# Column-normalised attention with a soft mixture of experts on one core: two PSUM sums of squares, seven more split tiles, another written order

## The chip, the cores and the metric

One Trainium2 chip, one core of it. The metric is device time in microseconds (us) of one launch. Five engines work beside each other and are named as in the profile: PE (TensorE, matmuls; PEld is its weight load), DVE (VectorE), ACT (ScalarE), POOL (GpSimd) and SP (SyncE, which here issues every DMA).

## The reference

Four batches of 5056 tokens with 256 channels, all fp32. Attention is over the channels: the columns of q and k are normalised over the tokens, and their product is a 256 x 256 matrix per batch. The result of all batches goes through a soft mixture of 8 experts with 4 slots each.

```python
qn = q / (np.linalg.norm(q, axis=1, keepdims=True) + 1e-06)
kn = k / (np.linalg.norm(k, axis=1, keepdims=True) + 1e-06)
s = kn.transpose(0, 2, 1) @ qn / tau
a = softmax(s, axis=-1)
x = (v @ a).reshape(20224, 256)
logits = x @ phi                      # 32 slots
d = softmax(logits, axis=0)           # over all tokens
slot_input = d.T @ x                  # 32 x 256
h = np.maximum(slot_input[e] @ w1[e], 0.0);  slot_out[e] = h @ w2[e]
c = softmax(logits, axis=1)
out = c @ slot_out
```

x is never formed: per batch, M = a @ phi gives the logits as v @ M, and the slots are gathered as (d.T @ v) @ a.

## The kernel before

**Tiling.** q and k of a batch come in 10 units (u = 0 to 39 over the four batches) of up to four tiles of 128 tokens; a unit is one 1 MB load, `raw`. A tile j of a unit goes one of two ways. As it is, it costs PE one fp32 product per half of the columns (L316, `S<-raw`). Split (j below `NS[u]`), ACT casts it to fp32r (L271, `hl<-raw`), POOL subtracts the cast from the original for the rest (L275), and PE makes three fp32r products per half (L322, `S<-hl`). Before, NS splits 108 tiles: none of unit 0, two in units 1 to 9, three in all later ones. ACT also squares the whole unit (L279, `sq<-raw`), and DVE adds the squares of all tiles of a batch in one PSUM bank, `A` (L286 for the first add of two tiles, then L298), the last add going to SBUF as `nsum` (L296). PE sums `nsum` over the partitions (L335, `nn`), and the norms, the scaled scores, their exponentials `a` and M follow on DVE, POOL, ACT and PE.

v comes in 20 pairs p (five a batch, one 1 MB load each). The logits need v transposed, `x`: for the pairs in `LT` it is loaded a second time in turned form (1 MB, L454), for the other seven PE turns v in 16 transposes (L459, `T`) and ACT copies the four banks to `x` (L464). PE makes the logits (L479, `L`), running maxima go over DVE and PE, and PE gathers v with the weights into the slots (L593, `G`). After the last batch come the experts (L742 `H`, L760, L775 `O`) and then the output: PE (L813), copies by ACT and DVE (L830) into 21 MB of stores by SP (L834 to L839).

**What sets the order.** Every step is a Python function put into the list `plan`; `ORDER` is a permutation of that list, written out by hand, and `run(plan)` calls the steps in that order. Each engine executes its instructions in just this order; semaphores make one wait for another. `SLOTS` gives every large tile one of 22 SBUF buffers of 1 MB, `BANKS` every PSUM tile one of 8 banks. A load or a step that takes a buffer waits until the tile that had it before has been read for the last time, and everything behind it on its engine waits with it. SP issues the loads in one queue, so a load that waits holds up the ones behind it.

`constants` makes the identity on POOL, a few constants and the sums `fold`, `fold4` from the identity on DVE (L231, L233), and a first Exp on ACT (`warm`). It stands 18th in the order before: POOL makes the identity after its first two subtractions.

Of the kernel before, what the change touches and what calls it, by code (L numbers as in the profile page):

```python
# [24 lines left out]
NT = [3 if u % (2 * UB) == 2 * UB - 1 else 4 for u in range(NU)]  # L25

NS = [0, 2, 2, 2, 2, 2, 2, 2, 2, 2, 3, 3, 3, 3, 3, 3, 3, 3, 3, 3, 3, 3, 3, 3, 3, 3, 3, 3, 3, 3, 3, 3, 3, 3, 3, 3, 3, 3, 3, 3]

LT = {0, 1, 2, 3, 4, 5, 6, 7, 8, 9, 10, 11, 12}
# [6 lines left out]

ORDER = [
# [130 lines left out]
def colnorm_attention_soft_moe(  # L168
# [112 lines left out]
    def add(u, j):  # L281
        b, i = divmod(u, UB)
        s = sqs[u].rearrange("p j x c -> p j (x c)")
        if i == 0 and j == 1:
            st[b]["acc"] = bank(f"A{b}")
            dve.tensor_tensor(st[b]["acc"], s[:, 0], s[:, 1], op=ALU.add)  # L286
            return
        r = slice(0, P)
        if j == 3 and i == UB - 1:
            r = slice(0, HD)  # L290
        elif j < 0:
# [767 lines left out]
```

## Time and profile before

| what | us |
|---|---|
| runs of the kernel | 302.66, 303.75, 623.18 (median 303.75) |
| the profiled execution, its own time | 302.02 |
| its span, first to last instruction | 300.1 |
| PE / DVE / ACT / POOL busy in the span | 256.4 / 222.1 / 201.7 / 143.5 |
| data moved | 113.96 MB, 92.57 MB of it read |

The span falls in three parts: the inputs with all of the attention up to some 227 us, the experts to some 245, and the output to the end. A row of the profile names line, engine, operation, the tile written and those read; "waits" are idle stretches of an engine, put down to what ended them. A line number is that of the kernel printed above.

### The profile page before, as it was taken

The page shows a single profiled execution, that of the slowest core. Times are in us where ns is not written, and L with a number is a line of the kernel's source. Part 1 is how long each engine was busy: PE and PEld are TensorE (multiplying, and loading weights), DVE is VectorE, ACT ScalarE, POOL GpSimd, SP SyncE. Part 2 cuts the span into 40 slices and gives each one's busy share as a digit, 9 for nine tenths or more (in the row PEclk, how much of TensorE's full clock was granted, in tenths as well). Part 3 has the DMA queues.
Part 4 walks back from the last instruction along what each step waited for, and adds up shares of the span by engine and source line. Part 5 has one row for each costly group of instructions (what it writes and reads, how often), then busy time and mean ns, then how long its engine had stood idle before and what let it go on. Part 6 is the DMA issues. An engine that isn't in the chain of part 4 may idle for free.

```text
span 300.1 us, 6394 instructions
## 1 busy us (share of the span) xinstructions
PE 256.4 (85%) x2526; PEld 202.9 (68%) x2526; DVE 222.1 (74%) x432; ACT 201.7 (67%) x302; POOL 143.5 (48%) x118
## 2 busy tenths in 40 slices
PE   5699799998999996999799988999989999997000
PEld 3498699997777885986667776877753777764000
DVE  0299489899948799999999999938889447884200
ACT  2995998959888995966878761859733327675000
POOL 0678699995797998777947963000000000000000
PEclk9999899999999999999999999999997999999555
DMA  7999999999999999999999999999993019999996
GB/s 286 425 425 421 420 419 330 340 405 371 428 421 420 416 425 424 420 412 418 418 421 423 419 420 419 419 421 420 420 420 128 2 72 382 415 416 417 419 423 264
DMA packets 16446, 113.96 MB, mean 380 GB/s; under 512 B 1952, under 2 KB 1952, under 8 KB 3488
## 3 DMA queue, kind: packets, MB, share of 16 engines
q1 hardware_dynamic: 16416, 113.55, 92.2%
q8 instruction: 20, 0.33, 0.4%
q14 instruction: 10, 0.08, 0.1%
HBM read 92.57 MB, written 20.97 MB: 378 GB/s over the span
## 4 chain that ended last, share of the span: by engine, by line
PE 39%; DVE 18%; POOL 16%; issue 9%; ACT 8%; DMA 2%; SPq 0%; DVEq 0%; POOLq 0%; ACTq 0%
POOL hl L275 15%; DVE A L298 9%; PE op_None L813 6%; PE S L322 5%; ACT sq L279 5%; PE G L593 4%; PE T L459 4%; PE L L479 4%; PE H L742 3%; PE S L316 3%; PE O L775 3%; PE op L813 2%; DMA raw<-in_qk_dram 2%; ACT hl L271 2%; ACT o L830 1%
## 5 line engine op out<-in xcount | busy, mean ns | idle before, releaser
L275 POOL TENSOR_TENSOR hl<-raw,hl 128x512 fp32r<-128x512 f32 x108 | 139.0, 1323 | 36.0 <-ACT hl L271 36.0
L298 DVE TENSOR_TENSOR A<-sq,A 128x512 f32<-128x512 f32 (+1 forms) x148 | 101.6, 691 | 10.1 <-ACT sq L279 5.6
L322 PE MATMUL S<-hl 128*128 128x256 f32 x648 | 93.5, 295 | 2.0 <-POOL hl L275 1.3
L322 PEld LDWEIGHTS S<-hl 128*128 128x128 f32 x648 | 83.0, 192 | 9.2 <-issue 4.9
L279 ACT ACTIVATE sq<-raw 128x2048 f32<-128x2048 f32 (+1 forms) x40 | 75.2, 1888 | 7.9 <-DVE A L298 5.3
L316 PE MATMUL S<-raw 128*128 128x256 f32 (+1 forms) x208 | 55.7, 403 | 6.5 <-DMA raw<-in_qk_dram 6.5
L271 ACT CAST hl<-raw 128x1024 fp32r<-128x1024 f32 (+1 forms) x69 | 56.4, 855 | 3.4 <-PE S L316 1.2
L316 PEld LDWEIGHTS S<-raw 128*128 128x128 f32 (+1 forms) x208 | 38.2, 198 | 15.6 <-DMA raw<-in_qk_dram 8.7
L830 DVE COPY o<-op_None 128x512 f32<-128x512 f32 x30 | 19.1, 685 | 6.9 <-PE op_None L813 5.9
L813 PE MATMUL op_None<-so,cT 32*128 32x256 f32 x240 | 23.0, 411 | 1.0 <-ACT o L830 0.6
L593 PE MATMUL G<-v,dn 128*32 128x256 f32 x312 | 19.5, 382 | 3.5 <-DVE dn L573 3.1
L830 ACT COPY o<-op_None 128x512 f32<-128x512 f32 x30 | 16.0, 593 | 7.4 <-PE op_None L813 7.0
L813 PEld LDWEIGHTS op_None<-so,cT 32*128 32x128 f32 x240 | 16.1, 183 | 7.1 <-ACT o L830 4.0
L479 PE MATMUL L<-x,M 128*32 128x256 f32 (+1 forms) x320 | 20.3, 380 | 0.4 <-ACT M L424 0.4
L593 PEld LDWEIGHTS G<-v,dn 128*32 128x32 f32 x312 | 10.4, 109 | 9.6 <-issue 3.6
L464 ACT COPY x<-T 128x512 f32<-128x512 f32 x28 | 14.9, 604 | 2.3 <-PE T L459 2.3
L502 ACT COPY lt<-L 128x256 f32<-128x256 f32 x20 | 7.1, 380 | 12.1 <-PE L L479 10.2
L459 PE MATMUL T<-ident,v 128*128 128x128 f32 x108 | 14.0, 276 | 0.0
L459 PEld LDWEIGHTS T<-ident,v 128*128 128x128 f32 x108 | 11.9, 141 | 2.0 <-issue 1.5
L479 PEld LDWEIGHTS L<-x,M 128*32 128x32 f32 x320 | 9.2, 109 | 6.0 <-ACT M L424 0.9
L830 DVE COPY oh<-op 128x256 f32<-128x256 f32 x20 | 7.3, 416 | 4.7 <-PE op L813 4.6
L563 ACT ACTIVATE lt<-lt,negm 128x256 f32<-128x256 f32 (+2 forms) x11 | 7.5, 682 | 4.8 <-DVE negm L547 4.7
(113 smaller groups left out, 249.2 us busy)
## 6 DMA issues: line engine op xcount, KB each, us to landing
raw<-in_qk_dram SPq DMA_DIRECT2D x37, 1024.0 KB, 12.9
v<-in_v_dram SPq DMA_DIRECT2D x16, 1024.0 KB, 10.7
w<-in_moe_w_dram SPq DMA_DIRECT2D x16, 1024.0 KB, 12.6
out_dram<-o SPq DMA_DIRECT2D x15, 1024.0 KB, 12.7
x<-in_vt_dram SPq DMA_DIRECT2D x13, 1024.0 KB, 11.8
out_dram<-oh SPq DMA_DIRECT2D x4, 1024.0 KB, 5.8
v<-in_v_dram SPq DMA_DIRECT2D x4, 896.0 KB, 12.9
raw<-in_qk_dram SPq DMA_DIRECT2D x2, 768.0 KB, 9.3
```

The source lines that it names most:

```text
L271: act.copy(parts(u, lo, hi)[:, :, 0::2, :], raws[u][:, lo:hi])
L275: pool.tensor_tensor(hl[:, :, 1::2, :], raws[u][:, lo:hi], hl[:, :, 0::2, :].bitcast(F32), op=ALU.subtract)
L279: act.activation(sqs[u][:, : NT[u]], raws[u][:, : NT[u]], AF.Square)
L298: dve.tensor_tensor(a[r], s[r, j], a[r], op=ALU.add)
L316: pe.matmul(sm, raw[r, j, 1, cols], raw[r, j, 0, :], start=first, stop=False, skip_group_check=True)
L322: pe.matmul(sm, hl[:, w, cols], hl[:, y, :], start=first, stop=False, skip_group_check=True)
L459: pe.transpose(tp[:, P * jj : P * jj + P], vtile(p, 4 * h + jj)[:, P * m : P * m + P], ident)
L464: to(xt(p)[:, m, h * UT : h * UT + UT], tps[p, h, m])
L479: pe.matmul(L[S * g : S * g + S, :n, :], M[:, m, :], x[:, :n, S * g : S * g + S], start=m == 0 and g not in void, stop=m == 1, skip_group_ ...
L593: pe.matmul(gp[S * g : S * g + S, :C], dn[:, x, j, :], vtile(p, j), start=x == 0 and j < G, stop=x == n - 1 and j >= G,)
L813: pe.matmul(ops[b, p, hf, g][:, h, :], cT[b][r, 4 * i : 4 * i + 4, :].rearrange("s j t -> s (j t)"), rhs[r], start=True, stop=True,)
L830: (dve.tensor_copy if g % 2 else act.copy)(dst, ops[b, p, hf, g])
```

## The change

- **Two sums.** The squares of the even and odd tiles of a batch are added in two PSUM banks, `A<b>_0` and `A<b>_1`. In the batch's ninth unit the odd sum goes to SBUF (`nsum<b>_odd`, in the same buffer as `nsum` and `aT`), and a new step `join` adds it to the even one. The last unit's tiles all go to the even bank. There are 156 such additions on DVE before and after.
- **Constants first.** `constants` stands second in the order, behind one load.
- **Split tiles.** NS is 0, 2, 2 and then 3 throughout: 115 tiles split instead of 108. The seven are in units 3 to 9.
- **Pairs.** LT holds the pairs 2 to 14 instead of 0 to 12: 13 turned loads as before, but PE turns the pairs 0 and 1 (and 15 to 19) instead of 13 and 14 (and 15 to 19).
- **Order.** ORDER, SLOTS and BANKS are other tables throughout; the gathers keep their bank under a key of batch and group.

```diff
-NS = [0, 2, 2, 2, 2, 2, 2, 2, 2, 2, 3, 3, 3, 3, 3, 3, 3, 3, 3, 3, 3, 3, 3, 3, 3, 3, 3, 3, 3, 3, 3, 3, 3, 3, 3, 3, 3, 3, 3, 3]
+NS = [0, 2, 2, 3, 3, 3, 3, 3, 3, 3, 3, 3, 3, 3, 3, 3, 3, 3, 3, 3, 3, 3, 3, 3, 3, 3, 3, 3, 3, 3, 3, 3, 3, 3, 3, 3, 3, 3, 3, 3]
-LT = {0, 1, 2, 3, 4, 5, 6, 7, 8, 9, 10, 11, 12}
+LT = {2, 3, 4, 5, 6, 7, 8, 9, 10, 11, 12, 13, 14}
 ORDER = [
-    1, 8, 3, 2, 9, 4, 25, 12, 35, 26, 29, 34, 28, 22, 51, 64, 38, 0, 5, 116, 27, 90, 77, 60, 103, 13, 15, 23,
+    37, 0, 1, 3, 7, 2, 38, 42, 39, 48, 41, 40, 10, 4, 5, 52, 54, 53, 6, 63, 44, 57, 9, 56, 24, 11, 82, 67,
...
     def add(u, j):
...
-        if i == 0 and j == 1:
-            st[b]["acc"] = bank(f"A{b}")
-            dve.tensor_tensor(st[b]["acc"], s[:, 0], s[:, 1], op=ALU.add)
+        if i == 0 and j in (1, 3):
+            st[b]["acc", j // 2] = bank(f"A{b}_{j // 2}")
+            dve.tensor_tensor(st[b]["acc", j // 2], s[:, j - 1], s[:, j], op=ALU.add)
             return
-        r = slice(0, P)
+        r, x = slice(0, P), j % 2 if i < UB - 1 else 0
...
-        a = st[b]["acc"]
-        if i == UB - 1 and j == 2:
+        a = st[b]["acc", x]
+        if i == UB - 2 and j == 3:
+            st[b]["odd"] = bpool.tile([P, 2 * C], F32, tag="nsum", name=f"nsum{b}_odd")
+            dve.tensor_tensor(st[b]["odd"], s[:, j], a, op=ALU.add)
+        elif i == UB - 1 and j == 2:
...
+    def join(b):
+        a = st[b]["acc", 0]
+        dve.tensor_tensor(a, st[b]["odd"], a, op=ALU.add)
...
-    at(-2, constants)
+    at(-9, constants)
...
+        if i == UB - 1:
+            at(u + 0.39, join, b)
```

In the rows of the order below, a name's last number only tells tiles of one program apart; `raw3_93` is the load of unit 3, `sq3` its squares, `A0_0` the even sum of batch 0.

**The start of DVE.** The first instructions behind the memsets, before:

```order
L231 TENSOR_REDUCE fold_81<-ident_72 128x32
L233 COPY fold4_82<-fold_81 128x32 x4
L286 TENSOR_TENSOR A0_139<-sq0_102 128x512
L298 TENSOR_TENSOR A0_139<-sq2_143,A0_139 128x512
L298 TENSOR_TENSOR A0_139<-sq0_102,A0_139 128x512
L298 TENSOR_TENSOR A0_139<-sq1_162,A0_139 128x512
L298 TENSOR_TENSOR A0_139<-sq4_167,A0_139 128x512 x3
L298 TENSOR_TENSOR A0_139<-sq1_162,A0_139 128x512
```

and now:

```order
L230 TENSOR_REDUCE fold_81<-ident_72 128x32
L232 COPY fold4_82<-fold_81 128x32 x4
L285 TENSOR_TENSOR A0_0_131<-sq0_129 128x512
L285 TENSOR_TENSOR A0_1_138<-sq0_129 128x512
L300 TENSOR_TENSOR A0_0_131<-sq3_125,A0_0_131 128x512
L300 TENSOR_TENSOR A0_0_131<-sq2_170,A0_0_131 128x512
L300 TENSOR_TENSOR A0_0_131<-sq4_155,A0_0_131 128x512
L300 TENSOR_TENSOR A0_0_131<-sq3_125,A0_0_131 128x512
L300 TENSOR_TENSOR A0_1_138<-sq4_155,A0_1_138 128x512
L300 TENSOR_TENSOR A0_0_131<-sq4_155,A0_0_131 128x512
L300 TENSOR_TENSOR A0_1_138<-sq4_155,A0_1_138 128x512
L300 TENSOR_TENSOR A0_1_138<-sq6_210,A0_1_138 128x512
```

The sums from the identity stay in front of the first add on DVE; what moved is the identity itself, which POOL now makes before all subtractions. Of the first ten additions before, all but the first read the sum that the one in front of them wrote; now the chain is broken where `A0_1` stands between two of `A0_0`. Over the whole program an addition stands directly behind one whose result it reads 103 times before and 54 times now.

**The start of ACT.** The first instructions before:

```order
L279 ACT_TABLE_LOAD
L279 ACTIVATE sq0_102<-raw0_93 128x2048
L271 CAST hl1_110<-raw2_104 128x4x256
L230 ACTIVATE warm_77<-ones_73 128x1
L279 ACTIVATE sq2_143<-raw2_104 128x2048
L271 CAST hl0_153<-raw1_106 128x4x256
L279 ACTIVATE sq1_162<-raw1_106 128x2048
```

and now:

```order
L229 ACT_TABLE_LOAD
L229 ACTIVATE warm_77<-ones_73 128x1
L270 CAST hl2_117<-raw3_93 128x4x256
L270 CAST hl3_120<-raw3_93 128x2x256
L278 ACTIVATE sq3_125<-raw3_93 128x2048
L278 ACTIVATE sq0_129<-raw0_110 128x2048
L270 CAST hl4_135<-raw4_133 128x4x256
```

The table load and `warm` stand in front of everything that needs data, and the first work is the cast of unit 3, not the square of unit 0. Up to the copy of batch 0's score matrix S0 out of PSUM (`ssb`, L330), ACT has 16 squares, 16 casts of two tiles and 8 of one before; now 15 squares, 15 casts of two tiles, 12 of one and 3 copies of turned v. Behind that copy PE has 77 split tiles, 23 whole ones and 28 banks of transposes before; now 83, 21 and 22.

**PE in front of unit 27.** `raw27` takes a buffer over. Before, it is the buffer of `hl23`, whose last reader is `S1<-hl23` 36 rows ahead of `S2<-raw27` in PE's order; the rows that lie last ahead of `raw27` are:

```order
L593 MATMUL G0_0_957<-v2_654,dn0_0_923 32x256 x8
L322 MATMUL S2_870<-hl28_988 128x256 x6
L322 MATMUL S2_870<-hl29_906 128x256 x6
L316 MATMUL S2_870<-raw26_816 128x256 x2
L322 MATMUL S2_870<-hl27_1029 128x256 x6
L316 MATMUL S2_870<-raw25_784 128x256 x2
L322 MATMUL S2_870<-hl31_996 128x256 x6
L322 MATMUL S2_870<-hl30_994 128x256 x6
L316 MATMUL S2_870<-raw27_821 128x256 x2
```

Now the buffer is that of `v1`, whose last reader is the gather in the first of these rows:

```order
L599 MATMUL G0_0_1027<-v1_309,dn0_0_1025 32x256 x8
L599 MATMUL G0_0_1027<-v2_720,dn0_0_1025 32x256 x8
L328 MATMUL S2_845<-hl28_939 128x256 x6
L328 MATMUL S1_373<-hl27_821 128x256 x6
L328 MATMUL S2_845<-hl33_1059 128x256 x6
L328 MATMUL S2_845<-hl31_1091 128x256 x6
L328 MATMUL S2_845<-hl27_821 128x256 x6
L328 MATMUL S2_845<-hl28_939 128x256 x6
L531 MATMUL rp0_1_1155<-ident_72,mx0_1_1151 1x128
L328 MATMUL S1_373<-hl26_827 128x256 x6
L322 MATMUL S2_845<-raw27_1110 128x256 x2
```

The same holds in kind for the loads of units 20 to 28: between the step that frees the buffer and the first step that needs the new load there is less work on PE than before. (For unit 27 it is now the gather of v2's pair, seven split tiles and one small matmul.)

## Rows read from the trace of the kernel before

**Rows 1.** The page's busy time, share of the span and instructions of each engine, and of its 40 slices (7.5 us each) the busy tenths of the DMA engines and their GB/s.

```profile
PE 256.4 (85%) x2526; PEld 202.9 (68%) x2526; DVE 222.1 (74%) x432; ACT 201.7 (67%) x302; POOL 143.5 (48%) x118
...
DMA  7999999999999999999999999999993019999996
GB/s 286 425 425 421 420 419 330 340 405 371 428 421 420 416 425 424 420 412 418 418 421 423 419 420 419 419 421 420 420 420 128 2 72 382 415 416 417 419 423 264
```

**Rows 2.** Busy time of each engine in four stretches of the span (us from its start; in brackets the number of instructions), granted clock, DMA share, GB/s.

```profile
10.00:62.00 52.00, 48.20 (x293) 42.92 (x291) 40.82 (x61) 45.85 (x38) 45.48 (x38) 0.97 0.99 396
...
190.00:227.00 37.00, 35.79 (x438) 25.78 (x440) 28.75 (x85) 24.64 (x66) 0.00 (x0) 0.99 1.01 417
227.00:245.00 18.00, 18.00 (x326) 10.68 (x322) 9.29 (x18) 6.37 (x12) 0.00 (x0) 0.93 0.04 16
245.00:300.00 55.00, 29.69 (x426) 22.14 (x414) 26.34 (x52) 21.46 (x49) 0.00 (x0) 0.79 0.93 383
```

**Rows 3.** The page's chain that ended last: shares of the span by engine and by line.

```profile
PE 39%; DVE 18%; POOL 16%; issue 9%; ACT 8%; DMA 2%; SPq 0%; DVEq 0%; POOLq 0%; ACTq 0%
POOL hl L275 15%; DVE A L298 9%; PE op_None L813 6%; PE S L322 5%; ACT sq L279 5%; PE G L593 4%; PE T L459 4%; PE L L479 4%; PE H L742 3%; PE S L316 3%; PE O L775 3%; PE op L813 2%; DMA raw<-in_qk_dram 2%; ACT hl L271 2%; ACT o L830 1%
```

**Rows 4.** The same chain in order of time: start in us, us, what.

```profile
28.78 4.16 issue
...
225.24 1.39 DVE cm L687
226.79 8.39 PE H L742 x64
```

**Rows 5.** ScalarE in order of time: start, us, line, operation, out<-in, count, and in brackets the idle time before it and what ended it.

```profile
5.71 1.28 ACT L279 ACT_TABLE_LOAD   x1 [5.71 <-DMA raw<-in_qk_dram]
7.01 1.91 ACT L279 ACTIVATE sq<-raw 128x2048 f32<-128x2048 f32 x1
...
28.25 3.71 ACT L279 ACTIVATE sq<-raw 128x2048 f32<-128x2048 f32 x2 [3.44 <-DVE A L298]
...
62.33 0.65 ACT L330 COPY ssb<-S 128x256 f32<-128x256 f32 x2 [1.53 <-PE S L316]
```

**Rows 6.** VectorE in order of time, columns as in the group before.

```profile
12.98 0.38 DVE L231 TENSOR_REDUCE fold<-ident 128x32 f32<-128x128 f32 x1 [11.75 <-POOL ident masks.py:199]
13.40 2.18 DVE L233 COPY fold<-fold 128x32 f32<-128x32 f32 x4
15.49 0.69 DVE L286 TENSOR_TENSOR A<-sq 128x512 f32<-128x512 f32 x1
16.29 15.56 DVE L298 TENSOR_TENSOR A<-sq,A 128x512 f32<-128x512 f32 x21
...
137.66 0.68 DVE L296 TENSOR_TENSOR nsum<-sq,A 128x512 f32<-128x512 f32 x1
138.25 0.69 DVE L298 TENSOR_TENSOR A<-sq,A 128x512 f32<-128x512 f32 x1
...
178.16 5.13 DVE L298 TENSOR_TENSOR A<-sq,A 128x512 f32<-128x512 f32 x7
```

**Rows 7.** Groups of instructions by line, engine, operation and shape: count, busy us, mean ns of one, idle us of the engine before them and what ended it.

```profile
L275 POOL TENSOR_TENSOR hl<-raw,hl 128x512 fp32r<-128x512 f32 x108 | 139.0, 1323 | 36.0 <-ACT hl L271 36.0
L298 DVE TENSOR_TENSOR A<-sq,A 128x512 f32<-128x512 f32 x144 | 98.9, 691 | 10.0 <-ACT sq L279 5.6
L322 PE MATMUL S<-hl 128*128 128x256 f32 x648 | 93.5, 295 | 2.0 <-POOL hl L275 1.3 <-ACT hl L271 0.6
...
L279 ACT ACTIVATE sq<-raw 128x2048 f32<-128x2048 f32 x38 | 72.2, 1910 | 7.9 <-DVE A L298 5.3 <-POOL hl L275 1.2 <-PE S L322 0.9
L316 PE MATMUL S<-raw 128*128 128x256 f32 x192 | 51.3, 403 | 6.5 <-DMA raw<-in_qk_dram 6.5
L271 ACT CAST hl<-raw 128x1024 fp32r<-128x1024 f32 x39 | 40.2, 1041 | 3.4 <-PE S L316 1.2 <-DVE A L298 1.1 <-issue 0.5
...
L593 PE MATMUL G<-v,dn 128*32 128x256 f32 x312 | 19.5, 382 | 3.5 <-DVE dn L573 3.1 <-issue 0.4
...
L271 ACT CAST hl<-raw 128x512 fp32r<-128x512 f32 x30 | 17.7, 614 | 0.0
...
L464 ACT COPY x<-T 128x512 f32<-128x512 f32 x28 | 14.9, 604 | 2.3 <-PE T L459 2.3
L459 PE MATMUL T<-ident,v 128*128 128x128 f32 x108 | 14.0, 276 | 0.0
```

**Rows 8.** Who waited for whom: us in total, times, longest.

```profile
PE G L593 <- DVE dn L573: 3.1, 2, 2.5
...
PE rp L525 <- DVE mx L520: 1.9, 1, 1.9
...
PE nn L335 <- DVE nsum L296: 1.3, 2, 0.8
```

**Rows 9.** The page's DMA issues (KB each, median us from issue to landing), and the first store in SP's own order of time.

```profile
raw<-in_qk_dram SPq DMA_DIRECT2D x37, 1024.0 KB, 12.9
...
out_dram<-oh SPq DMA_DIRECT2D x4, 1024.0 KB, 5.8
...
245.52 0.35 SPq L839 DMA_DIRECT2D out_dram<-oh  x1
```

**Rows 10.** PE in order of time, columns as in rows 5: the products that make the slots.

```profile
225.31 1.31 PE L671 MATMUL slp<-gts,a 128*128 128x32 f32 x8
```

More of the change, by code (lines that the diff above doesn't have):

```diff
@@ L588, in gather @@
         if x == 0:
-            st[b]["gp"] = bank(f"G{b}_{gi}")
-        gp, dn = st[b]["gp"], dns[b, gi]
+            st[b]["gp", gi] = bank(f"G{b}_{gi}")
+        gp, dn = st[b]["gp", gi], dns[b, gi]
         for j in range(8):
@@ L601, in finish_evict @@
     def finish_evict(b, gi):
-        gp = st[b]["gp"]
+        gp = st[b]["gp", gi]
         if gi == 0:
@@ L865, in colnorm_attention_soft_moe @@
             at(u - 0.5 + 0.1 * j, low, u, j, j + 1)
-        js = [1, 2, 3] if i == 0 else [0, 1, 3, 2] if i == UB - 1 and b % 2 == 0 else list(range(NT[u]))
+        js = [1, 3] if i == 0 else [0, 1, 3, 2] if i == UB - 1 and b % 2 == 0 else list(range(NT[u]))
         if i == 0 and b % 2:
```

231 rows, old and new, of tables (BANKS, ORDER, SLOTS) are left out of this document.

## Prediction, made blind

> **What bounds the kernel now.** I read the busy table and the slices of the page first. No engine is full over the span: PE 85%, DVE 74%, ACT 67%, POOL 48%; but the DMA engines run at 420 GB/s in most slices [rows 1]. 113.96 MB at that rate are 271 us of a span of 300.1 us. What is missing lies in three places: a start, a dip in slices 7 to 10 (330, 340, 405, 371 GB/s), and a hole of some 18 us after the inputs, where DMA stands at 0.04 while PE does the experts [rows 1, 2]. The hole is the one that counts: the output can't start before the experts are through, and it then streams for the rest of the span. The first store goes out at 245.52 and the span ends 54.6 us later [rows 9]; H starts at 226.79 [rows 4], 18.7 us before that store. So the time is the start of H plus 73.3 us, as long as the experts and the output keep their shape. The question is when H starts.
>
> Then the chain of waits, by share and in order of time. PE has 39%, DVE 18%, POOL 16%, ACT 8%, and 9% are issue [rows 3]. In time it is first POOL (subtractions with gaps), then DVE and PE by turns, and towards the end PE: from 190 to 227 us it is busy 35.79 of 37.00 us [rows 2]: there only less work on PE, or an earlier arrival at 190, helps. Up to 62 us it is different: POOL waited 36.0 us in all for the casts of ACT [rows 7], ACT is busy 45.85 of 52 us [rows 2], and ACT's one long gap, 3.44 us in front of 28.25, waits for additions on DVE, which still hold the buffer of the squares [rows 5]. DVE is late because it starts late: its first add is at 15.49, behind a wait of 11.75 us for the identity of POOL and 2.6 us for `fold` [rows 6]. The chain shows it as 4.16 us of issue at 28.78, between two stretches of POOL [rows 4].
>
> **The change part by part.** All terms are against the profiled execution: 302.02 us, 1.9 above its span. The median of the runs shown is 303.75, 0.6% more.
>
> *First stage (to the copy of S0 at 62.33 [rows 5]).* With the identity made first, DVE can add as soon as unit 0 is squared: by the new order that is behind one wide and one narrow cast and two squares, 5.7 + 1.0 + 0.6 + 1.9 + 1.9 = 11.1 us (the first 1 MB was there at 5.71) with the durations of [rows 5, 7], 4.4 us earlier than 15.49. That is more than the 3.44 us that ACT waited, so I let this wait go: -3.4. The table load, 1.28 us in front of the first square [rows 5], no longer waits for data: -1.3. ACT's own list changes by one square less, one wide cast less, four narrow casts more and three copies more: -1.91 - 1.04 + 4 x 0.614 + 3 x 0.604 = +1.3 [rows 7]. Together -3.4. Bounds: 0, if ACT meets another wait at once, and -6.2, if all its 52 - 45.85 us of idle time went [rows 2].
>
> *Two sums.* A run of seven adds to one sum takes 5.13 us [rows 6] and one alone 0.69 [rows 7], so they start 0.74 us apart; the 21 early ones give 0.74 too. Where an add follows that doesn't need the one before, `nsum` at 137.66 and an add of the next batch at 138.25, it starts after 0.59 [rows 6]. A result that is needed at once thus costs 0.15 us here, and 49 fewer additions are in that place (103 to 54): 7.2 us of DVE. DVE's adds are 9% of the chain, 27 us of some 99 us of them [rows 3, 7], so about 27% of it is on the path: -1.9. Bounds: 0 and -7.2.
> The Trainium skill says the opposite (VectorE: DVE Perf Modes, "The DRAIN you can't avoid"): after each DVE operation the pipe empties before the next starts, whether or not it needs the result, and only the number of operations counts. That number is 156 both times, so by the rule this term is 0. The trace doesn't agree where it shows both cases, 0.59 against 0.74 us; but these are few places, so the rule's case is kept as a rival below.
>
> *Split and turned tiles.* Behind the first stage PE has six split tiles more at 93.5/108 = 0.87 us, two whole ones less at 51.3/48 = 1.07 and six banks of transposes less at 14.0/27 = 0.52 [rows 7]: 5.2 - 2.1 - 3.1 = 0.0. PE thus has as much to do as before; the two turned pairs have left the tail, but other work of the same size is now behind S0. POOL gets 7 x 1.32 = 9.3 us more [rows 7]; it is idle for far longer, behind ACT, and that idle time is the cover. If it fell on the path by POOL's share of the chain (16%) it would cost 1.5; I take +0.3.
>
> *Buffers and loads.* The new tables let a load wait for a buffer that is freed late. For unit 27, one gather (16 instructions a pair, 19.5 us for 312 [rows 7]: 1.0 us) and seven split tiles, 1.0 + 7 x 0.87 = 7.1 us of PE work, now lie between the buffer's last reader and the first product with the new data, where 36 rows of PE lay before. A 1 MB load lands 12.9 us after its issue in the median, with others in front of it, and a 1 MB transfer took 5.8 us where the queue was short [rows 9]. So such a place costs 0 with a short queue and up to 12.9 - 7.1 = 5.8 us with a full one. Units 20 to 28 are built like this. Since the loads there come one by one, I take the short end: +1.5, with 0 and +17 (three rounds of 5.8) as bounds. PSUM has one bank less for everything but A; the price is in the same bounds.
>
> *A new wait.* The odd sum of the third batch has to wait on DVE until PE has read `aT` of the second; `join` and the additions of the next unit stand behind it. The nearest rows are waits of PE for DVE of 0.8 to 2.5 us [rows 8]; bounds 0 and +2.5, I take +0.3. *Tail:* `c_max` ([rows 4]) now stands behind the copy that H needs, but PE's slot products (225.31 + 1.31 [rows 10]) end together with it (225.24 + 1.39), so 0; the output half 0 is now finished before half 1 is begun, which makes the first store some 1 us later and the next ones denser: +0.2, bounds -1 and +2.
>
> Sum: -3.4 - 1.9 + 0.3 + 1.5 + 0.3 + 0.2 = -3.0, so 302.0 - 3.0 = 299.0 us, 1.0% under the profiled execution and 1.6% under the median. A measurement of this kernel can tell about 2%, 6 us, from no change: the borders are 297.7 and 309.8.
>
> **The rivals.**
> - *A larger gain.* DVE is the engine behind most waits of PE: 3.1 for the weights, 1.9 for the maxima, 1.3 for `nsum` [rows 8], 6.3 us. If all of the 7.2 us of DVE came off the path, through these waits, and the loads held up: 302.0 - 3.4 - 7.2 + 0.3 + 0.5 = 292.2. For it: DVE carries 18% of the chain. Against: PE has hardly a gap behind 190 us.
> - *Loads on the path; slower.* Place: units 20 to 28, some 65 to 105 us; price: 5.8 us each time that PE waits for a load issued behind its own last step. It decides from the third round: with the other terms (-3.0 - 1.5 = -4.5) 302.0 - 4.5 + 17.4 = 314.9; two rounds give 309.1, still in the band. For it: DMA already dips in slices 7 to 10 [rows 1], and the distance for unit 27 is a fraction of what it was. Against: two turned loads fewer come early, and the load of one unit is 2.5 us at 420 GB/s.
> - *Nothing gained.* The adds cost the same in two banks (the rule above), and what DVE gives back to ACT in the first stage is lost to the casts and copies that come earlier: 302.0 - 1.3 + 1.3 + 0.5, about 302. For it: ACT is nearly full there. Against: the rows on both kinds of adds.
>
> **How the numbers follow.** Forecast 36%, larger gain 30%, nothing gained 20%, loads on the path 14%. The forecast's own range is 295 to 302; about a fifth of it lies below 297.7. Faster by over 2%: 0.30 + 0.07 = 0.37. Slower by over 2%: the loads alone, 0.14. Within 2%: the rest, 0.49. The range reaches to the larger gain's 292 and, towards two rounds of late loads, to 308: 291.5 to 308.
>
> **What would show it.** First add on DVE near 11 us, no wait of ACT for DVE before 30 us, S0 copied by 59 to 60: first stage right. Runs of additions in two banks starting 0.59 to 0.62 us apart, those in one bank 0.74: the second term right; all at 0.74: wrong, and the rule right. Waits of PE, ACT or POOL for `raw` after 60 us: if more than 6 us in all, the loads' rival. H before 222: the larger gain. Wrong altogether if H starts after 230, or if the time from H to the end moves by more than 3 us from 73.3.

## The result and the profile after

The changed kernel takes 0.965 of the time before (95% interval 0.960 to 0.970): 10.7 us less of 303.7. Profile against profile it is 302.02 to 292.82 us, 9.2 less; 3.0 was forecast. The four listed times are 292.59, 292.82, 297.96 and 301.6; the ratio leaves out executions that were disturbed, as do all below, and the traces of experiments 2, 3, 4, 11, 14 and 17 come from such longer executions, so that only single instructions are read from them.

In the tables below the span is cut at three marks: the end of the copy of S0, the first product with the last batch's `nsum` (`nn3`), and the first product of `H`. Busy time of the engines between the marks, before and after (us of the stretch, then each engine's busy us and count, clock, DMA share, GB/s):

```profile
62.98:184.41 121.43, 112.78 (x994) 92.48 (x992) 110.16 (x199) 96.32 (x128) 95.80 (x75) 1.00 1.01 417
184.41:226.79 42.38, 41.17 (x485) 30.07 (x485) 33.96 (x98) 26.77 (x71) 1.01 (x1) 0.99 1.01 418
```

```profile
58.39:178.40 120.01, 114.35 (x1013) 96.76 (x1012) 111.70 (x200) 103.00 (x138) 104.21 (x82) 1.00 0.99 399
178.40:216.95 38.55, 37.80 (x468) 28.55 (x468) 31.80 (x92) 21.62 (x61) 2.29 (x1) 0.96 1.01 421
```

So the first stage is 4.6 us shorter, the middle 1.4, the tail from `nn3` to H 3.8, and from H to the end it is 0.8 longer (73.3 before, 291.0 - 216.95 = 74.05 after): 9.1 of span. Look at PE in the second rows: it is nearly full in both, 41.17 of 42.38 and 37.80 of 38.55. The tail is shorter and PE has 3.4 us less to do there; experiments 10 and 13 test that the one comes from the other. In the first rows PE has 1.6 us more to do and the stretch is still shorter, since PE's idle time falls from 8.65 to 5.66.

The page after, busy time and chain; they answer to [rows 1, 3]:

```profile
PE 250.6 (86%) x2540; PEld 205.4 (71%) x2540; DVE 220.8 (76%) x432; ACT 204.4 (70%) x309; POOL 154.1 (53%) x125
...
PE 33%; DVE 24%; ACT 13%; POOL 10%; DMA 8%; issue 4%; DVEq 0%; POOLq 0%
DVE A L300 11%; POOL hl L274 9%; PE op_None L819 7%; PE S L328 6%; ACT hl L270 5%; ACT sq L278 5%; DMA raw<-in_qk_dram 4%; DMA v<-in_v_dram 4%; PE H L748 3%; PE L L485 3%; PE T L465 3%; PE op L819 3%; PE O L781 3%; PE G L599 2%; PE S L322 1%
```

DVE after, in order of time, against [rows 6]: the first addition stands at 10.88 instead of 15.49, and a run of 24 additions takes 15.84 us, 0.66 each, where a run to one sum went at 0.74.

```profile
10.88 1.30 DVE L285 TENSOR_TENSOR A<-sq 128x512 f32<-128x512 f32 x2 [8.70 <-ACT sq L278]
...
21.48 15.84 DVE L300 TENSOR_TENSOR A<-sq,A 128x512 f32<-128x512 f32 x24 [1.55 <-ACT sq L278]
```

Yet DVE's busy time is only 1.3 us less. Its groups after show one reason (count, busy us, mean ns): the first additions of a batch, eight now and four before, read two SBUF buffers and take 1239 ns in the mean, 8 x 0.55 = 4.4 us more than eight of the other kind; the four of before (1054 ns) cost 1.5 us more than four of the other kind.

```profile
L300 DVE TENSOR_TENSOR A<-sq,A 128x512 f32<-128x512 f32 x132 | 86.4, 689 | 7.9 <-ACT sq L278 5.8
...
L285 DVE TENSOR_TENSOR A<-sq 128x512 f32<-128x512 f32 x8 | 9.8, 1239 | 9.4 <-ACT sq L278 9.4
```

PE's waits for DVE between S0 and H, against [rows 8]: 6.3 us for the three kinds before, 3.1 now.

```profile
PE rp L531 <- DVE mx L526: 1.3, 1, 1.3
...
PE nn L341 <- DVE nsum L298: 1.1, 1, 1.1
...
PE G L599 <- DVE dn L579: 0.7, 1, 0.7
```

### The profile page after: what moved, and what is told of

It reads as the page before. It is cut to its first block, busy times and chain, and to the rows that moved or that the text cites. A ratio compares the mean times of both kernels' runs of the same rounds, so it can differ in the third digit from the quotient of the medians.

```text
span 291.0 us, 6435 instructions
## 1 busy us (share of the span) xinstructions
PE 250.6 (86%) x2540; PEld 205.4 (71%) x2540; DVE 220.8 (76%) x432; ACT 204.4 (70%) x309; POOL 154.1 (53%) x125
## 4 chain that ended last, share of the span: by engine, by line
PE 33%; DVE 24%; ACT 13%; POOL 10%; DMA 8%; issue 4%; DVEq 0%; POOLq 0%
DVE A L300 11%; POOL hl L274 9%; PE op_None L819 7%; PE S L328 6%; ACT hl L270 5%; ACT sq L278 5%; DMA raw<-in_qk_dram 4%; DMA v<-in_v_dram 4%; PE H L748 3%; PE L L485 3%; PE T L465 3%; PE op L819 3%; PE O L781 3%; PE G L599 2%; PE S L322 1%
## 5 line engine op out<-in xcount | busy, mean ns | idle before, releaser
L274 POOL TENSOR_TENSOR hl<-raw,hl 128x512 fp32r<-128x512 f32 x115 | 148.2, 1325 | 22.7 <-ACT hl L270 22.4
L328 PE MATMUL S<-hl 128*128 128x256 f32 x690 | 98.5, 293 | 0.1
L300 DVE TENSOR_TENSOR A<-sq,A 128x512 f32<-128x512 f32 (+1 forms) x136 | 89.2, 689 | 8.1 <-ACT sq L278 5.8
L328 PEld LDWEIGHTS S<-hl 128*128 128x128 f32 x690 | 87.6, 190 | 6.0 <-issue 3.2
L270 ACT CAST hl<-raw 128x1024 fp32r<-128x1024 f32 (+1 forms) x76 | 60.6, 833 | 6.9 <-DMA raw<-in_qk_dram 5.8
L322 PE MATMUL S<-raw 128*128 128x256 f32 (+1 forms) x180 | 46.8, 394 | 6.5 <-DMA raw<-in_qk_dram 6.4
L322 PEld LDWEIGHTS S<-raw 128*128 128x128 f32 (+1 forms) x180 | 32.8, 196 | 11.7 <-DMA raw<-in_qk_dram 6.8
L285 DVE TENSOR_TENSOR A<-sq 128x512 f32<-128x512 f32 x8 | 9.8, 1239 | 9.4 <-ACT sq L278 9.4
L514 DVE TENSOR_REDUCE mxs<-L 128x1 f32<-128x256 f32 x20 | 7.8, 408 | 3.9 <-PE L L485 2.2
L518 DVE STREAM_TRANSPOSE nat<-L 128x256 f32<-128x256 f32 x20 | 8.5, 435 | 1.7 <-PE L L485 1.7
## 6 DMA issues: line engine op xcount, KB each, us to landing
out_dram<-o SPq DMA_DIRECT2D x15, 1024.0 KB, 11.1
```

Source lines behind the costliest of these rows:

```text
L270: act.copy(parts(u, lo, hi)[:, :, 0::2, :], raws[u][:, lo:hi])
L274: pool.tensor_tensor(hl[:, :, 1::2, :], raws[u][:, lo:hi], hl[:, :, 0::2, :].bitcast(F32), op=ALU.subtract)
L300: dve.tensor_tensor(a[r], s[r, j], a[r], op=ALU.add)
L322: pe.matmul(sm, raw[r, j, 1, cols], raw[r, j, 0, :], start=first, stop=False, skip_group_check=True)
L328: pe.matmul(sm, hl[:, w, cols], hl[:, y, :], start=first, stop=False, skip_group_check=True)
```

## The experiments

Times are ratios to the kernel before, each measured beside it on one chip (1 to 4, 5 to 8, 9 to 12, 13 to 16 and 17 on chips of their own), with 95% intervals; a difference of 0.01 is 3.0 us, and a difference of two kernels here is good to some 1.5 to 2 us. "Changed" is the changed kernel (0.965). Where a trace is used, the last four columns are its stretches in us, cut as above. They belong to one execution each, so their sum need not move by just what the ratio says.

| kernel | ratio | interval | S0 copied | to `nn3` | to H | to the end |
|---|---|---|---|---|---|---|
| before | 1 | | 63.0 | 121.4 | 42.4 | 73.3 |
| changed | 0.9648 | 0.960-0.970 | 58.4 | 120.0 | 38.6 | 74.1 |
| 1 before, constants first | 0.9884 | 0.985-0.992 | 61.1 | 121.5 | 43.9 | 72.0 |
| 2 changed, constants later | 0.9651 | 0.961-0.969 | | | | |
| 3 changed, one bank | 0.9780 | 0.973-0.983 | | | | |
| 11 the same again | 0.9721 | 0.968-0.976 | | | | |
| 4 changed, first squares in PSUM | 0.9552 | 0.952-0.959 | | | | |
| 5 and no shared reads | 0.9469 | 0.943-0.950 | 57.9 | 118.1 | 37.0 | 73.6 |
| 6 as 5, one bank | 0.9455 | 0.942-0.949 | 57.9 | 117.0 | 37.0 | 75.4 |
| 7 before, no shared reads | 0.9706 | 0.967-0.974 | 64.5 | 113.2 | 43.8 | 72.1 |
| 9 as 7, constants first | 0.9649 | 0.961-0.969 | 60.3 | 113.2 | 43.8 | 73.3 |
| 8 as 5, 7 us more of DVE | 0.9523 | 0.949-0.956 | 57.8 | 120.6 | 36.8 | 72.4 |
| 10 as 5, 13 and 14 turned too | 0.9694 | 0.965-0.974 | 58.1 | 117.1 | 47.6 | 72.1 |
| 12 as 5, seven tiles whole | 0.9693 | 0.965-0.974 | 63.3 | 117.0 | 36.8 | 74.0 |
| 13 as 5, turned pairs as before | 0.9683 | 0.964-0.973 | 60.4 | 116.5 | 41.7 | 72.5 |
| 17 changed, turned pairs as before | 0.9906 | 0.987-0.995 | | | | |
| 14 changed, short operations only | 0.9512 | 0.948-0.955 | | | | |
| 15 as 14, one bank | 0.9475 | 0.944-0.951 | 57.9 | 117.5 | 36.7 | 73.0 |
| 16 before, attention's three only | 0.9812 | 0.978-0.985 | 63.6 | 116.2 | 43.1 | 72.2 |

**Experiments 1, 2 and 9: the constants.** In the order of before, and in the changed one, step 0 is moved:

```diff
 ORDER = [                      # 1 (and 9): before
-    1, 8, ..., 64, 38, 0, 5,
+    1, 0, 8, ..., 64, 38, 5,
 ORDER = [                      # 2: changed
-    37, 0, 1, 3, 7, 2, 38, 42, 39, 48, 41, 40,
+    37, 1, 3, 7, 2, 38, 42, 39, 48, 41, 0, 40,
```

> The kernel before with one edit: the step `constants` second in the written order instead of eighteenth. One bank, 108 split tiles, everything else as before. Theory (first stage): DVE's first add moves from 15.49 to about 11, ACT's 3.44 us wait in front of 28.25 and the 1.28 us of the table load go, S0 is copied at about 58 instead of 62.33, and all that follows shifts with it: 302.0 - 3.4 to - 4.3, so 298 (ratio 0.986). Rival (ACT is full there and meets its next wait at once, the gain of the changed kernel's first stage is its new written order): S0 at 61.5 or later, 301 to 302.

> The changed kernel with `constants` put back behind the first two subtractions of POOL (place 10 instead of 1). Theory (first stage): DVE's first add behind 15, ACT waits for it again, S0 copied about 3.4 to 4.3 later than 58.02, the end by as much later: 292.8 + 3.4 to 4.3, some 296.7. Rival (the new order is what shortens the first stage): S0 within 1 us of 58.02, 292.5 to 294.

> The kernel of the seventh experiment with `constants` second in the written order, as in the first. Theory (the first stage's gain is DVE's earlier start and adds to the rest): 3.5 us less than the seventh, 291. Rival (given back behind S0, as the trace of the first experiment shows: -1.9 us at S0's copy, -0.4 at H): 293.5 to 294.6.

Early constants are worth 3.5 us in the kernel before, as expected, though S0 is copied only 1.9 us earlier, at 61.0 instead of the 58 of my theory. They are worth 1.7 (0.9706 to 0.9649) once its short operations are out of the way, where 3.5 was expected; in the changed order their place is worth nothing, which is the rival. There POOL's first two subtractions come so early (7.05 us in experiment 2, 9.93 before) that the identity isn't late: the first addition of experiment 2 stands at 11.23, against 10.88. So DVE's early start is worth 1.7 to 3.5 us in the order of before, and the new order gives it by itself.

**Experiments 3 and 11: one bank.** The odd tiles are added to `A<b>_0` (a batch's first unit in three additions), `join` does nothing, and the odd sum is not copied out.

```diff
...
-        r, x = slice(0, P), j % 2 if i < UB - 1 else 0
+        r, x = slice(0, P), 0
...
```

> The changed kernel with the odd tiles added into the even tiles' bank (one sum, no join, 3 additions for a batch's first unit as before, no wait for aT), all else as changed. Theory (the shorter chains of dependent adds are what took 3.4 us from PE's idle time behind S0): additions again 0.73 to 0.75 us apart in runs, DVE some 7 us fuller in the adds that follow one another but 4 two-buffer first adds less, PE's idle time between S0's copy and H back from 6.4 to 9 or more: 295 to 297. Rival (the written order and the turned pairs did that, the DVE is covered): within 1 us of 292.8.

> The kernel of the third experiment once more, for a trace of one of its shorter executions: 295.6 to 297. Theory (two banks are worth nothing by themselves, fifth against sixth; here one bank moves short operations of DVE into POOL's runs): rn, rk, sm, al, zacc, rowrun together take some 4 us more than the changed kernel's. Rival (the adds): these stay within 1 us, and PE, ACT or POOL wait some 4 us more for nsum and the additions.

The time says that two banks are worth 4.0 us in one measurement and 2.2 in the other, the second barely clear of the noise, as my theory had it. Experiments 6 and 15 show that the theory is wrong all the same.

**Experiments 4 and 5: operations that read SBUF twice, beside POOL.** ACT writes two squares of each batch's first unit into the sums, and then the short operations are changed too.

```diff
...
+        act.activation(st[b]["acc", y], raws[UB * b][:, 2 * y].rearrange("p x c -> p (x c)"), AF.Square)
...
-            dve.tensor_tensor(st[b]["acc", j // 2], s[:, j - 1], s[:, j], op=ALU.add)
...
+                dve.tensor_tensor(st[b]["acc", y], s[:, j], st[b]["acc", y], op=ALU.add)
     # 5, besides:
-        dve.tensor_scalar_add(sm, sm, 1e-9)
-        dve.tensor_scalar_add(rn, rn, 1e-6)
-        dve.tensor_scalar_mul(rk, st[b]["rn"][:, 2:4], rtau)
+        act.mul(rk, st[b]["rn"][:, 2:4], rtau)
...
-            dve.tensor_tensor(al, negm, now["negm"], op=ALU.subtract)
...
-        act.activation(als[b, gi], als[b, gi], AF.Exp)
+        act.activation(als[b, gi], olds[b, gi], AF.Exp, bias=negms[b, gi], scale=-1.0)
...
```

> The changed kernel where ACT writes the squares of tiles 0 and 2 of a batch's first unit straight into the two sums (three instructions in place of one, for four units), so that DVE's 8 first additions read one buffer and the bank instead of two buffers. Theory (a first addition with two buffers is stretched while POOL subtracts, 1.24 us in the mean against 0.67): the 8 take about 0.67 each, 4.6 us of DVE less, of which about a third is on the path, against some 1.5 us more of ACT: 291 to 292.5. Rival (nothing there is on the path, ACT's extra overhead is, in the first stage): 293 to 294.

> The kernel of the fourth experiment, and besides none of DVE's short operations beside POOL reads two SBUF buffers or scales one in SBUF: the terms 1e-9 on `sm` and 1e-6 on `rn` are left out (sums of 1 and more, which such a term doesn't change in float32), `rk`, `al`, `be` and `zacc` go to ACT, `row` is kept in PSUM. Theory (such an operation waits for POOL's running subtraction and, where POOL has the next one ready, for several: 0.6 to 1.3 us each against 0.17 idle, and 10.4 us once in the trace of the fourth): about 8 us of DVE go, at least a third of that from the path: 285 to 288, and its executions lie within 1.5% of each other. Rival (short operations behind which nobody waits): 290 +- 1, with executions of 298 and more as before.

Experiment 4 takes 2.9 us off, 5 another 2.5, and the six times of 5 lie between 285.60 and 288.55, as its theory had it. What such an operation waits for is seen best in the trace of experiment 4, in DVE's rows and then in POOL's (start, us):

```profile
59.79 10.37 DVE L356 TENSOR_SCALAR sm<-sm 128x2 f32<-128x2 f32 x1
70.20 0.17 DVE L357 RECIPROCAL sm<-sm 128x2 f32<-128x2 f32 x1
```

```profile
56.42 13.72 POOL L216 TENSOR_TENSOR hl<-raw,hl 128x512 fp32r<-128x512 f32 x11
```

An operation on two numbers a partition lasts until POOL's run of eleven subtractions is over, 70.16 against 70.14. The reciprocal behind it, on the same numbers, takes 0.17. In the kernel before, such a wait is one subtraction long: DVE's `sm` and POOL's run,

```profile
112.16 1.23 DVE L393 TENSOR_SCALAR sm<-sm 128x2 f32<-128x2 f32 x1
113.42 0.17 DVE L394 RECIPROCAL sm<-sm 128x2 f32<-128x2 f32 x1
```

```profile
110.81 5.06 POOL L275 TENSOR_TENSOR hl<-raw,hl 128x512 fp32r<-128x512 f32 x4 [0.23 <-ACT hl L271]
```

whose second subtraction ends at about 110.81 + 2 x 1.265 = 113.34, with `sm` at 113.39. POOL goes on with the third at once, and the reciprocal runs beside it. The groups of before for `rn`, `sm` and `al` carry the waits in their means (their shortest are 0.16, 0.17 and 0.16 us):

```profile
L551 DVE TENSOR_TENSOR al<-negm,negm 128x1 f32<-128x1 f32 x7 | 3.4, 479 | 0.2
...
L349 DVE TENSOR_SCALAR rn<-rn 128x4 f32<-128x4 f32 x4 | 3.2, 802 | 0.2 <-POOL rn L345 0.2
...
L393 DVE TENSOR_SCALAR sm<-sm 128x2 f32<-128x2 f32 x4 | 2.5, 627 | 3.7 <-ACT a L383 3.7
```

The Trainium skill (SBUF — State Buffer, "Who interferes with whom") states the rule: a DVE operation with two SBUF inputs contends with a GpSimd operation that reads SBUF, one in a two-port mode with any, and one side waits for the whole instruction of the other. The traces agree in that the waiting operations end with a subtraction; that `sm` and `rn`, which read one buffer, run in a two-port mode is shown by no run here. How many subtractions such an operation waits for differs: in the kernel before `sm` got its turn between two of them, in experiment 4 it waited for eight. What decides it isn't shown.

**Experiments 7, 14 and 16: the short operations alone,** in the kernel before, in the changed one, and in the kernel before `rn`, `sm` and `rk` only; the edits are those of 5.

> The kernel before with the short operations changed as in the fifth experiment (its 4 first additions still read two buffers). They took 0.8, 0.63, 0.48 us (rn, sm, al) against 0.16 to 0.17 at their shortest, about 7 us of DVE. Theory (DVE's time is on the path to a larger share than the 27% of the chain): 299 to 301. By the 27%: 301.5 to 302. Rival (nobody waits): 303.5 to 304.

> The changed kernel with the short operations of the fifth experiment alone (terms of 1e-9 and 1e-6 left out; rk, al, be, zacc on ACT; row in PSUM); the 8 first additions read two buffers. Theory (short operations are worth 9 us in the kernel before, seventh experiment, and in the changed order only about 2.4, fifth against fourth): 290 to 290.5. Rival (they are worth as much here, the fourth had part of it): 286 or less.

> The kernel before with rn, sm and rk alone changed (the terms 1e-6 and 1e-9 left out, rk on ACT); al, be, zacc and row stay on DVE. Theory (an operation between a batch's sums and its M holds up all that follows, one between peaks and weights less): at least two thirds of the seventh's 9 us, 296 to 298. Rival (each counts by its length: 5.5 of some 10 us): 299.

They are worth 8.9 us before (expected 2 to 5) and 4.1 in the changed kernel (expected 2.4). In the trace of 7, whose span is 6.6 us shorter, the middle is 8.2 us shorter, 121.4 to 113.2, and the first stage and the tail are some 1.4 longer each. `rn`, `sm` and `rk` alone give 5.7, a little under the two thirds expected. They stand between a batch's sums and its M, where the logits wait. The experiments take these operations away or give them to ACT, so the gains hold their own time as well as their waits.

The new order loses about half as much to all of them, and not because they wait less. Added up over the traces of before and after, `rn`, `rk`, `sm`, `al`, `be`, `zacc` and `rowrun` take 16.2 us of DVE before and 17.8 in the changed kernel; each at its shortest, they would take 7.9 and 8.3. So less of that time holds up others in the new order; which part of the order does it isn't shown.

**Experiments 6, 15 and 8: the additions again.** Experiment 6 is 5 with one bank, 15 is 14 with one bank (the edit of 3; in 6, of the direct squares one per batch stays). Experiment 8 adds ten operations to 5:

```diff
...
             dve.tensor_tensor(a[r], s[r, j], a[r], op=ALU.add)
+            if j == 2 and u in (12, 13, 15, 18, 21, 24, 27, 33, 34, 36):
+                dve.tensor_scalar_mul(a, a, 1.0)
```

> The kernel of the fifth experiment with the odd tiles added into the even tiles' bank (one square straight into it per batch, no join). Theory (two banks: 49 additions less that wait for the one in front of them, 0.15 us each): 3 to 4 us slower than the fifth, as the third was than the changed kernel. Rival (what the third lost, it lost to waits for POOL): within 1 us of the fifth.

> The fourteenth with one bank, as in the third experiment. Theory (two banks are worth nothing by themselves): within 1 us of the fourteenth, or up to 1.5 less, since 4 first additions beside POOL go. Rival (the 0.15 us of 49 additions, 7.2 us, at the prediction's 27% or more): +2 to +4.

> The kernel of the fifth experiment with ten more operations on DVE, a multiplication of the even sum by 1 in PSUM (128x512, about 0.7 us) behind tile 2 of units 12, 13, 15, 18, 21, 24, 27, 33, 34 and 36: 7.3 us of DVE. By the 27% of the chain +2.0; theory (DVE's time behind the first stage is mostly on the path, 0.6 to 1): +4.4 to +7.3. Rival (covered): within 1 us.

One bank is as fast as two: 0.4 us faster in 6, 1.1 in 15, each within some 1.6 us. And it is not that the additions are alike. Experiment 5's run of 24 goes at 0.66 us, experiment 6's run of 28 at 0.74:

```profile
21.72 15.84 DVE L257 TENSOR_TENSOR A<-sq,A 128x512 f32<-128x512 f32 x24 [1.55 <-ACT sq L227]
```

```profile
21.66 20.66 DVE L250 TENSOR_TENSOR A<-sq,A 128x512 f32<-128x512 f32 x28 [1.16 <-ACT sq L225]
```

The time is saved on DVE, and the kernel isn't faster for it. Experiment 8 has a price for DVE's time: its ten operations took 7.0 us of DVE and cost 1.6 (0.0054), 23%, give or take some 1.5 us. That is far under the 60% and more of my theory and near the prediction's 27%. What experiments 3 and 11 lost goes away with the short operations; how one bank makes these dearer is not shown. In the traces of 3 and 11 one `sm` takes 10.27 and 10.25 us, like the 10.37 of 4.

**Experiments 10, 13 and 17: the turned pairs.** Experiment 10 turns 13 and 14 with PE as well; 13 puts back all of that part of the change (0 and 1 loaded, v of 14 loaded earlier); 17 does the same in the changed kernel.

The edit in words (the steps stand in `ORDER`, and the eight banks of the transposes in `BANKS`):

```diff
+    turn(p, h, m), turned(p, h, m) for p in 13, 14, between load_v 14 and logits 14
-    load_vt 13, load_vt 14
-    turn, turned of pairs 0 and 1       # 13 and 17 only
+    load_vt 0, load_vt 1                # 13 and 17 only, where their first `turned` stood
```

> The kernel of the fifth experiment with pairs 13 and 14 turned by PE, as before, in place of their loads (pairs 0 and 1 still turned too): 8 banks of transposes, 4.2 us of PE, and 8 copies, 4.8 us of ACT, behind the last unit's scores, and 2 MB less to load. Theory (behind 178 us PE is the bound, so what leaves or enters there counts in full, and in the first stage it doesn't): +3.5 to +4.5, some 292. Rival (PE's work counts the same everywhere, and the smaller load pays for some of it): +2 or less.

> The kernel of the fifth experiment with the turned pairs as before the change: pairs 13 and 14 turned by PE in the tail, pairs 0 and 1 loaded turned; v of pair 14 is loaded ahead, in the place of the load that goes, so that the tenth experiment's wait of 3.2 us for it is gone. Theory (work of PE behind nsum of the last batch counts in full, in front of it PE has gaps that take some of it): from that nsum to H 5 us or more longer, up to it shorter by less, the whole +2 to +4, 290 to 292. Rival (the prediction's step: PE's work moved, so nothing changes): 288 +- 1.

> The changed kernel itself with the turned pairs as before: 13 and 14 turned in the tail, 0 and 1 loaded, as in the thirteenth experiment, which was made on a kernel without the short operations. Theory (the place of the turned pairs is the larger part of what the prediction missed): 6.5 us slower than the changed kernel, some 299. Rival (the waits for POOL take the difference up, or PE's work counts the same everywhere): 294 or less.

Putting the pairs back costs 6.5 us in the kernel of 5 (0.9469 to 0.9683; expected 2 to 4) and 7.8 in the changed one (expected 6.5). Experiment 10 cost 6.8, more than the 4.5 of its theory: in its trace the tail is 10.5 us longer than in 5, with a wait of 3.2 us for v and 6.9 us more of PE's busy time, at a granted clock of 0.93 there against 0.99. The stretches behind S0 in 5, then in 13:

```profile
57.88:176.02 118.14, 113.93 (x1013) 96.44 (x1011) 101.47 (x188) 104.25 (x149) 101.63 (x81) 1.00 1.00 403
176.02:213.03 37.01, 36.37 (x469) 28.27 (x469) 29.57 (x78) 23.89 (x67) 2.29 (x1) 0.99 1.01 419
```

```profile
60.44:176.98 116.54, 113.98 (x1004) 95.67 (x1003) 101.34 (x188) 101.99 (x144) 101.52 (x80) 1.00 1.00 410
176.98:218.66 41.68, 40.58 (x501) 31.20 (x501) 29.60 (x78) 28.23 (x75) 2.29 (x1) 1.00 1.00 414
```

In the tail PE is nearly full in both and has 4.2 us more to do in 13, and the tail is 4.7 longer. S0 comes 2.6 us later: 2 MB of v now stand in the queue ahead of q and k, and the waits for `raw` grow (below). The middle is 1.6 us shorter and the end 1.0, so these two traces are 4.6 us apart, less than the ratio's 6.5. That the transposes of pairs 0 and 1 cost nothing where they stand is argued, not measured alone: half of their stretch is the first stage of 5, where PE is idle for 7.1 of 57.88 us. The waits for `raw` in the first 60 us of 5 and of 13:

```profile
PE S L279 <- DMA raw<-in_qk_dram: 6.5, 1, 6.5
...
ACT hl L212 <- DMA raw<-in_qk_dram: 4.1, 2, 3.5
```

```profile
PE S L280 <- DMA raw<-in_qk_dram: 10.1, 5, 6.3
...
ACT hl L213 <- DMA raw<-in_qk_dram: 7.6, 4, 3.5
```

What the change itself did with the transposes is one more view, PE's `T` alone in the three stretches, before and then after (us of the stretch, PE busy and count, clock, DMA share, GB/s):

```profile
0.00:62.98 62.98, 0.00 (x0) 0.97 0.97 384
62.98:184.41 121.43, 0.00 (x0) 1.00 1.01 417
184.41:226.79 42.38, 14.23 (x112) 0.99 1.01 418
```

```profile
0.00:58.39 58.39, 3.49 (x24) 1.00 0.98 403
58.39:178.40 120.01, 3.33 (x24) 1.00 0.99 399
178.40:217.00 38.60, 8.19 (x64) 0.96 1.01 420
```

All 14.2 us stood in the tail; now 6.8 of 15.0 stand ahead of it, half of that in a first stage that is shorter all the same. Not all of it is the change of pairs: in 13, where the pairs are as before, 96 transposes stand in the tail and 16 ahead of it (112 and none before), so the new order alone moves these 16. What the pairs cost in 13 and 17 is their price within the new tables.

**Experiment 12: the split tiles.**

```diff
+    WHOLE = range(3, UB)
...
+        if u in WHOLE and lo == 2:
+            return
...
-        elif j >= NS[u]:
+        elif j >= NS[u] or (u in WHOLE and j == 2):
```

> The kernel of the fifth experiment with tile 2 of units 3 to 9 scored whole from raw, as before the change: 108 split tiles, POOL 7 subtractions (9.3 us) and ACT 7 parts of casts less, PE 7 x (1.07 - 0.87) = 1.4 us more. By the prediction's term the split tiles cost nothing either way: within 1 us of the fifth. Rival (POOL, nearly full up to 68 us, sets the first stage): S0's copy 1.5 us or more earlier and the time 1 to 2 us shorter.

It is 6.8 us slower by the ratio; in the traces, 4.5 us apart, S0 is copied 5.5 us later, 63.3 against 57.9, and the rest gives 0.9 back. That is neither my term nor the rival. ACT has a wait for PE there that experiment 5 doesn't have:

```profile
ACT sq L234 <- PE S L286: 6.2, 1, 6.2
```

That fits the buffers: a whole tile holds its `raw` until PE has read it, a split one only until ACT and POOL have, and the buffer tables are made for the second. So this is the price of the tile within these tables; what it is worth with others was not tried, and it can't be added to the prices of the other parts.

## Why the prediction was wrong

The sign was right; the sum was not. That 292.8 lies in the range is luck: the range reached so far down for the sake of the larger gain, whose mechanism did not happen (below).

One path of experiments leads from the kernel before to the changed one. Without the short operations (7) it is 8.9 us faster, with early constants (9) another 1.7. From there to 13, which has the banks, the split tiles, the direct squares and the tables of the new kernel but the old pairs, it is 1.0 slower. The turned pairs (13 to 5) take off 6.5, and with the short operations and the first additions back (5 to the changed kernel) 5.4 are lost again. So of the 10.7 us the pairs are 6.5, the constants 1.7, and 3.5 is what the new kernel loses less to short operations and first additions; the rest costs 1.0. Each step is good to some 1.5 us or 2, and the prices hang on the path: in the changed kernel itself the pairs are worth 7.8 (17), and the place of the constants nothing (2).

- **Split and turned tiles, +0.3: the step that failed.** I counted PE's work behind the first stage, found it equal, and wrote that the two turned pairs had left the tail "but other work of the same size is now behind S0". The count holds (153.96 to 152.15 us of PE from S0 to H). But a microsecond of PE isn't worth the same in all stretches. In the tail, where [rows 2] show 35.79 of 37.00 busy, it counts in full: 4.2 us more of it made the tail of 13 4.7 us longer, and in the change itself 3.4 us less go with a tail 3.8 us shorter. In the middle PE idled 8.65 us before. I had read the row of the tail and written that only less work on PE helps there, and then summed across the border. And that two turned loads fewer come early, 2 MB in a first stage whose DMA is full (0.97 before), stands in the prediction only as a word against a rival, without a price; S0 came 2.6 us later with them in 13. In place of +0.3 the pairs measure -6.5 (13) and -7.8 (17), within the new tables; what the seven split tiles are worth by themselves stays open (12).
- **Two sums, -1.9.** The two pitches, 0.59 or 0.66 and 0.74, were right (49 times 0.15 is 7.35, not 7.2, which hardly moves the term), and so, as far as the noise lets one say, was the share on the path (27% forecast, 23% measured). The gain still doesn't come: one bank is 0.4 and 1.1 us faster, each within some 1.6. What takes it back, the `join`, the second bank or the wait for `aT`, isn't shown. So the rival of nothing gained was right about this term alone. The Trainium skill's rule (VectorE: DVE Perf Modes, "The DRAIN you can't avoid") gives the right time, but not by what the prediction took from it, as the pitches differ; the same paragraph adds that an operation that is not held back starts earlier, which the prediction left out.
- **No term: the short operations.** They stood in the profile of before, `rn` at 0.80 us in the mean with 0.16 at the shortest, and the chain passes through them. I priced the additions, which are large, and passed over the short ones. Without them the kernel before is 8.9 us faster and the changed one 4.1 (7 and 14): the change loses 4.8 us less to them, and the sum had nothing for it. They didn't get shorter (16.2 to 17.8 us); why they cost less stays open.
- **First stage, -3.4.** The trace has -4.6. Early constants alone give -1.7 to -3.5 in the order of before and nothing in the new one; how the rest divides between the order and the two loads less isn't separated. The first addition came at 10.88 (11.1 forecast), and ACT no longer waited for DVE before 30 us.
- **Buffers and loads, +1.5.** Behind S0's copy the only wait for a load among the waits of the changed kernel is ACT's for `raw`, 1.9 us in all: about right in size, and under the 6 us that were the sign of the rival.
- **Larger gain, 292.2.** The time came out, and so did its sign, H before 222 (216.95), but the mechanism didn't: it had all of DVE's 7.2 us on the path, and experiments 6 and 15 find none of them in the time.

## What to carry to other kernels

Count an engine's work by stretch, not over the span, and price it by how full the engine is there: moving equal work from a full stretch into one with gaps can be a gain, although no total changes. Look at the mean of short operations against their shortest; five times as long was the mark of waits inside them here, where the table of waits shows nothing. Undoing one part of a change whose order and buffers were written for all of it prices that part within these tables only, and such prices don't add up. And when an experiment gives the expected number, undo the same thing once more in a kernel without the disturbing part before believing the reason.

## What the hardware showed beside that

- DVE operations that read two SBUF operands (`al`, the first additions) and scalings from SBUF to SBUF (`rn`, `sm`) take up to 1.8 us while POOL subtracts in the kernels before and after, against 0.12 to 0.67 at their shortest. Reciprocals of the same numbers (0.18 at most in the traces of before, after and 4) and additions with one operand in PSUM (0.69) don't show it.
- Such a wait can last for one subtraction (`sm` at 112.16 before, with POOL's next ones following at once) or to the end of a run of eleven (10.37 us in experiment 4). What decides isn't shown.
- Runs of additions that alternate between two PSUM banks have starts 0.59 to 0.66 us apart, those to one bank 0.74, at the same 0.69 us of duration. Whether the bank or the needed result makes the difference isn't separated.
